# Turning x earlier, loading q's last blocks last, and two passes of the last w_out in a fused attention and MLP kernel

## The chip, the cores and the metric

The kernel runs on one core of a Trainium2 chip. The time is that of one execution on the device in microseconds (us); medians are over the runs of one comparison. Ratios are the mean time of one kernel's runs over that of the other kernel's runs of the same rounds, so not quite the ratio of the medians that I quote. The granted TensorE clock (the share of full speed that the chip allowed) is quoted where it bears on a reading.

## The reference, cut to what matters

```python
# attention, per batch of 8 and head of 8, S = 576, D = 64
r = np.maximum(x, 0.0);  phi = concat([r * cos, r * sin], axis=-1)     # for q and for k
kv  = einsum('bhsf,bhsd->bhfd', k_p, v);  z = sum(k_p, axis=2)
num = einsum('bhsf,bhfd->bhsd', q_p, kv); den = q_p . z + 1e-6
x   = (num / den) transposed to 4608 tokens x 512
# MLP
h = x @ w_in                       # 512 x 2048
g = h * (1 / (1 + exp(-beta * h)))
return g @ w_out                   # 2048 x 512
```

## The kernel before: the parts that matter

The MLP runs in 9 chunks of 512 tokens, each of 32 slots: in slots 0 to 15 a first product h (four matmuls of 512 columns, 0.86 us) and its Silu, in slots 16 to 31 four matmuls of the second product o. The attention of a later batch runs between the slots. Chunk 0 shares its time with batch 1, chunk 1 with batch 2. A batch has 9 blocks of 64 rows times 2 groups of four heads (pairs 0 and 1 in the code). For batch 1 the first seven blocks go through TensorE during chunk 0, and the last two (blocks 7 and 8) in chunk 1. VectorE scales v by cos and sin (`vb`), rectifies q and k, and divides num (`xs`, called x below). Every engine works through its own instructions in program order.

```python
# start, batch 0, pair 1 (cuts marked ...)
    kv_mm(0, 1, 6)
    kv_take((1,), 6, eng="act")
    x_mul(got, 0, 7)
    x_mul_act(got2, 7)
    warm_pe(1, bank=1)                       # filler product
    for n in range(7):
        num_mm(n, 1, 0, n)
    num_mm(7, 1, 6, 0)                       # writes banks 6 and 7
    ...                                      # w_in 0 cast by GpSimd, half of it by VectorE below
    x_turn_pe(0, 0, 8, 2, jps=(0,))
    got = x_rden(0, 0, 0, 7, (1,))
    x_mul(got, 0, 4)
    x_mul(got, 4, 7)
    x_mul(x_rden(6, 0, 7, 8, (1,)), 7, 8)    # reads banks 6 and 7
    warm_pe(3, bank=3)
    x_turn_pe(0, 0, 4, 4, ("act",), (1,))
    h_mm(0, 0, (0, 1))
    x_turn_pe(0, 4, 8, 5, ("act",), (1,))
    for jt in range(1, 4):
        h_mm(0, jt, (0, 1))                  # jt 2 and 3 write banks 6 and 7
...
# what runs between the slots of a chunk, batch b
        u = [
            (0, lambda: num_rest() if b == 2 else None),     # batch 1's blocks 7 and 8
            (0, lambda: (q_relu(b, 0), q_relu(b, 1), q_turn_dma(b), load_next())),
            (1, lambda: v_scale(b, 0)),
            (4, lambda: k_relu(b)),
            (6, lambda: v_scale(b, 1)),
            (7, lambda: q_tan(b, 0)),
            (8, lambda: q_tan(b, 1)),
            (12, lambda: (kv_mm(b, 0, 6), kv_mm(b, 1, 6), kv_take((0, 1), 6))),
        ]
```

## Time and profile before

| | before |
|---|---|
| median of the first 3 runs | 296.25 us (296.04 to 296.49) |
| span of the profiled execution | 294.3 us |
| TensorE / VectorE / ScalarE / GpSimd busy | 284.1 / 116.6 / 140.1 / 73.8 us |
| slot 4 of chunk 0 starts | 22.21 us |
| chunk 1's first product | 51.59 us |
| kv product of batch 2 starts / the h after it | 64.52 / 65.66 us |

TensorE is the bound: it has next to no idle time after 16 us. The rest is read by asking what TensorE waits for at a few places; the prediction shows those lines. One caution on this trace: some matmul records are missing from it, 28 of 3074 by the page's count of products and weight loads.

### The profile page before, as it was taken

The numbers are of one execution on the slowest core, as the hardware profiler recorded it, in microseconds if no ns is written. First come the engines' busy times: TensorE is split into PE (matmuls) and PEld (weight loads), VectorE is DVE, ScalarE is ACT, GpSimd is POOL, SyncE is SP. The second block draws the span as 40 slices with busy tenths as digits, with TensorE's granted clock in tenths as the row PEclk, the third lists the DMA queues.
The fourth block names the chain that finished last, engine by engine and source line by source line (L and its number), as shares of the span: only waits on it lengthen the run. The fifth ranks groups of instructions, "written<-read, shape, count | busy, mean of one in ns | idle before, by whom it ended". The sixth has DMA issues, their size and how long they took to land.

```text
span 294.3 us, 7183 instructions
## 1 busy us (share of the span) xinstructions
PE 284.1 (97%) x3046; PEld 143.2 (49%) x3074; DVE 116.6 (40%) x297; ACT 140.1 (48%) x223; POOL 73.8 (25%) x88
## 2 busy tenths in 40 slices
PE   8799999999999999999999999999999999999995
PEld 7454455455444544454444544554455444444444
DVE  5989968662920294009500860077005000000000
ACT  5768826572248214831384128511761177127611
POOL 1350003252382026402460156014701210000000
PEclk9999999999999999999999999999999999999999
DMA  7999999597898089925992599239201910131033
GB/s 258 373 391 381 389 390 391 192 286 275 159 280 348 2 110 222 374 86 111 210 392 79 102 226 379 82 63 181 64 2 33 159 37 0 38 71 36 0 73 72
DMA packets 50416, 53.82 MB, mean 183 GB/s; under 512 B 30912, under 2 KB 31312, under 8 KB 50384
## 3 DMA queue, kind: packets, MB, share of 16 engines
q1 hardware_dynamic: 47424, 45.88, 51.7%
q0 software_dynamic: 2688, 7.34, 10.1%
q8 instruction: 24, 0.39, 0.5%
q10 hardware_dynamic: 272, 0.14, 0.2%
q14 instruction: 8, 0.07, 0.1%
HBM read 36.71 MB, written 9.44 MB: 157 GB/s over the span
## 4 chain that ended last, share of the span: by engine, by line
PE 84%; DVE 5%; DMA 5%; ACT 2%; issue 2%
PE ps L366 38%; PE ps L391 37%; DMA w_stage<-in_moe_w_out_dram 5%; DVE win L108 4%; PE ps L281 4%; PE ps L260 3%; PE ps L406 1%; PE ps L415 1%; ACT vb L213 1%; DVE qs L218 1%; DVE xs L303 0%; ACT g_t L373 0%; ACT rk L188 0%; PE ps L424 0%; PE ps L230 0%
## 5 line engine op out<-in xcount | busy, mean ns | idle before, releaser
L366 PE MATMUL ps<-xt,win 128*128 128x512 bf16 x576 | 128.1, 379 | 0.7 <-ACT g_t L373 0.5
L391 PE MATMUL ps<-wout,g_t 128*128 128x512 bf16 x535 | 120.4, 379 | 2.5 <-issue 1.4
L373 ACT ACTIVATE g_t<-ps,beta 128x512 bf16<-128x512 f32 x144 | 98.5, 688 | 36.5 <-PE ps L366 36.5
L366 PEld LDWEIGHTS <-win 128*128 128x128 bf16 x576 | 55.3, 98 | 67.5 <-DVE win L108 1.4
L391 PEld LDWEIGHTS <-g_t 128*128 128x128 bf16 x560 | 54.0, 98 | 64.0 <-issue 0.5
L386 POOL DMA_DIRECT2D out_dram<-o_sb x56 | 36.5, 656 | 142.2 <-ACT o_sb L397 142.2
L397 ACT COPY o_sb<-ps 128x512 f32<-128x512 f32 x35 | 20.5, 587 | 98.2 <-PE ps L391 98.2
L218 POOL TENSOR_TENSOR qs<-qt,tanr 128x1152 bf16<-128x1152 bf16 x12 | 29.2, 2456 | 10.3 <-DVE vb L215 8.9
L272 DVE CAST kv<-ps 128x520 bf16<-128x520 f32 x6 | 4.2, 699 | 67.8 <-PE ps L260 67.8
L409 DVE COPY o_sb<-ps 128x256 f32<-128x256 f32 (+1 forms) x2 | 0.7, 358 | 62.6 <-PE ps L406 62.6
L303 DVE TENSOR_TENSOR xs<-ps,rden 128x768 bf16<-128x768 f32 (+5 forms) x26 | 23.1, 890 | 0.8
L292 DVE TENSOR_TENSOR den<-ps,eps 128x12 f32<-128x12 f32 (+4 forms) x26 | 4.2, 161 | 33.5 <-PE ps L281 33.5
L215 DVE TENSOR_SCALAR vb<-raw_v,cos 128x256 bf16<-128x256 f32 x63 | 17.1, 348 | 0.0
L215 DVE TENSOR_SCALAR vb<-raw_v,sin 128x256 bf16<-128x256 f32 x54 | 14.7, 350 | 0.0
L281 PEld LDWEIGHTS <-qt 64*64 64x64 bf16 x576 | 10.6, 106 | 5.0 <-issue 4.3
L281 PE MATMUL ps<-kv,qt 64*64 64x65 bf16 x576 | 11.8, 194 | 0.4 <-ACT kv L270 0.2
L190 DVE TENSOR_SCALAR qb<-raw_q 128x1152 bf16<-128x1152 f32 x16 | 11.4, 753 | 1.3 <-DMA raw_q<-in_q_dram 1.3
L108 DVE CAST win<-w_stage 64x512 bf16<-64x512 f32 (+1 forms) x28 | 11.6, 413 | 0.6
L281 PE MATMUL ps<-kv,qs 64*64 64x65 bf16 x576 | 11.6, 193 | 0.0
L260 PE MATMUL ps<-vb,rk 64*64 64x130 bf16 x576 | 10.0, 218 | 1.6 <-ACT rk L188 1.6
L260 PEld LDWEIGHTS <-rk 64*64 64x64 bf16 x576 | 8.5, 106 | 5.6 <-issue 3.0
L281 PEld LDWEIGHTS <-qs 64*64 64x64 bf16 x576 | 10.4, 105 | 0.0
(56 smaller groups left out, 99.3 us busy)
## 6 DMA issues: line engine op xcount, KB each, us to landing
raw_v<-in_v_dram SPq DMA_DIRECT2D x7, 1152.0 KB, 10.3
raw_k<-in_k_dram SPq DMA_DIRECT2D x7, 1152.0 KB, 12.7
raw_q<-in_q_dram SPq DMA_DIRECT2D x7, 1152.0 KB, 7.5
out_dram<-o_sb POOLq DMA_DIRECT2D x56, 128.0 KB, 4.0
w_stage<-in_moe_w_out_dram SPq DMA_DIRECT2D x4, 1024.0 KB, 9.1
w_stage<-in_moe_w_in_dram SPq DMA_DIRECT2D x3, 1024.0 KB, 13.0
out_dram<-o_sb SPq DMA_DIRECT2D x14, 128.0 KB, 2.3
raw_q<-in_q_dram SPq DMA_DIRECT2D x2, 576.0 KB, 4.4
```

Of the source, the lines that this page charges most:

```text
L108: nc.vector.tensor_copy(o, a)
L190: nc.vector.tensor_scalar(dst, src, scalar1=0.0, scalar2=None, op0=ALU.max)
L215: nc.vector.tensor_scalar(o, a, scalar1=t[:, n : n + 1], scalar2=None, op0=ALU.mult)
L218: eng.tensor_tensor(dst.rearrange("q n (g p) -> q n g p", g=2), src.rearrange("q n (g p) -> q n g p", g=2), tanr[:, n0:n1].unsqueeze(2).to ...
L260: nc.tensor.matmul(t[jj * HP : (jj + 1) * HP, g], lhsT=rk[hs, n, 2 * jp + jj, :], rhs=vb[hs, n, 2 * jp + jj].rearrange("q s e -> q (s e)") ...
L281: nc.tensor.matmul(ps[cols, bank + jj, slot * E : (slot + 1) * E], lhsT=(qt, qs)[cs][rows, jp, n, cols], rhs=kv[rows, g, jp, cs, :], start ...
L303: nc.vector.tensor_tensor(o.rearrange("q j n s d -> q j (n s) d"), nv[:, :, a:z, :, 0:D].rearrange("q j n s d -> q j (n s) d"), rden[:, :, ...
L366: nc.tensor.matmul(ps[:, h_bank(c, jt)], lhsT=win[jt // 4][:, mi, (jt % 4) * P : (jt % 4 + 1) * P], rhs=xt[:, :, jp, g * HP : (g + 1) * HP ...
L373: nc.scalar.activation(g_t, ps[:, h_bank(c, jt)], AF.Silu, scale=beta[:, jt : jt + 1])
L386: eng.dma_start(out=out_v[bb, n][:, m0:m1], in_=o_sb[hf * HP : (hf + 1) * HP, m0:m1])
L391: nc.tensor.matmul(o_ps, lhsT=gs[c, jt][:, tt * P : (tt + 1) * P], rhs=wout[jt // 4][:, jt % 4, :], start=(jt == 0), stop=(jt == JT - 1))
L397: nc.scalar.copy(o_sb, o_ps)
```

## The change

The intent is to shorten the start and the transition to chunk 1, where TensorE waits. It has three parts: the start (A), the late blocks of batch 1's q (B) and the last w_out in two passes (C).

```diff
 # A: the start
-    v_scale(0, 1, 0, 0, 6, eng="pool")          # and the rest of the 9 blocks on ScalarE
+    v_scale(0, 1, 0, 0, 8, eng="pool")
...
-    warm_pe(1, bank=1)
+    x_turn_pe(0, 0, 8, 4, jps=(0,))             # ahead of num of pair 1
     for n in range(7):
         num_mm(n, 1, 0, n)
...
-    for gj in GJ:
-        cast_win(0, gj, "pool", jps=slice(0, 1))
...
-    x_turn_pe(0, 0, 8, 2, jps=(0,))
+    for gj, eng in zip(GJ, ("pool", "pool", "dve", "pool")):
+        cast_win(0, gj, eng, jps=slice(0, 1))
+    for gj, eng in zip(GJ, ("dve", "pool", "pool", "pool")):
+        cast_win(0, gj, eng, jps=slice(1, 2))
...
-    warm_pe(3, bank=3)
+    warm_pe(2, bank=3)
+    h_mm(0, 0, (0, 1))
+    h_mm(0, 1, (0, 1))
     x_turn_pe(0, 0, 4, 4, ("act",), (1,))
-    h_mm(0, 0, (0, 1))
+    h_mm(0, 2, (0, 1))
+    h_mm(0, 3, (0, 1))
     x_turn_pe(0, 4, 8, 5, ("act",), (1,))
...
+            if slot == 0:
+                for jt in range(4):
+                    h_mm(0, jt, (2, 3), slice(0, 4))   # left column half of all four h first
+            h_mm(0, slot, (2, 3), slice(4, 8))
-            h_mm(0, slot, (2, 3))
             h_act(0, slot)
 # B: the late blocks of batch 1's q
-        load_raw(1, "q")
+        load_raw(1, "q", n1=7)
         load_w("out", 3)
+        load_raw(1, "q", n0=7)
...
+        d = 4 if b == 2 else 0                          # every batch: slots 0, 1, 4, 6, 7, 8 become d + 0, 1, 3, 5, 6, 7
+        if b == 2:
+            u = [(0, lambda: (q_relu(1, 0, n0=7), q_relu(1, 1, n0=7))), (2, q_rest), (4, num_rest)] + u
 # C: the last w_out in two passes, slots 28 to 31 of chunk 0
+            for tt in (2 * (slot % 2), 2 * (slot % 2) + 1):
+                o_mm(0, tt, range(12, 14) if slot < 30 else range(14, 16))
...
-                     [takes[0](*t) for t in turns], cast_wout(3, "addd"),
+                     [takes[0](*t) for t in turns], cast_wout(3, "adda"),    # ScalarE casts its last part too
```

For batch 2 part B moves the units some four slots later. For every later batch, where d is 0, it also moves the last four one slot earlier (k's rectification, the sin half of `vb` and the two tan products, slots 3, 5, 6 and 7 instead of 4, 6, 7 and 8).

More of the change, by code (lines that the diff above doesn't have):

```diff
@@ L73, in raw_tile, with load_raw @@
         return raws[name, b]
-    def load_raw(b, name, j0=0, j1=4):
-        js = slice(j0, j1)
+    def load_raw(b, name, j0=0, j1=4, n0=0, n1=NQ):
+        js, nd = slice(j0, j1), slice(n0 * D, n1 * D)
         src = {"q": q, "k": k, "v": v}[name][b]
         nc.sync.dma_start(
-            out=raw_tile(b, name)[:, js].rearrange("q j n d -> q j (n d)"),
-            in_=src.rearrange("(j g) (p n) d -> (g p) j (n d)", g=2, n=NQ)[:, js, :])
+            out=raw_tile(b, name)[:, js].rearrange("q j n d -> q j (n d)")[:, :, nd],
+            in_=src.rearrange("(j g) (p n) d -> (g p) j (n d)", g=2, n=NQ)[:, js, nd])
     win = [const.tile([P, MI, 512], BF16, name=f"win{i}") for i in range(4)]
@@ L190, in relu, with q_relu @@
             nc.vector.tensor_scalar(dst, src, scalar1=0.0, scalar2=None, op0=ALU.max)
-    def q_relu(b, jp, eng="dve"):
-        relu(qb[:, jp].rearrange("q n (j d) -> q j n d", j=2), raw_tile(b, "q")[:, 2 * jp : 2 * jp + 2], eng)
+    def q_relu(b, jp, eng="dve", n0=0, n1=NQ):
+        relu(qb[:, jp, n0:n1].rearrange("q n (j d) -> q j n d", j=2),
+             raw_tile(b, "q")[:, 2 * jp : 2 * jp + 2, n0:n1], eng)
     def k_relu(b, j0=0, j1=4, eng="dve", n0=0, n1=NQ):
@@ L220, in tan_mul, with q_turn_pe @@
             tanr[:, n0:n1].unsqueeze(2).to_broadcast([P, n1 - n0, 2, HP]), op=ALU.mult)
-    def q_turn_pe(b, jp, bank, hold=False):
-        parts = ((0, 0, 5), (1, 5, NQ))
+    def q_turn_pe(b, jp, bank, hold=False, parts=((0, 0, 5), (1, 5, NQ))):
         v2 = []
@@ L360, in h_bank, with h_mm @@
         return ((3, 2, 6, 7), (2, 3, 0, 1))[c][jt] if c < 2 and jt < 4 else HB[jt % 4]
-    def h_mm(c, jt, mis=range(4)):
+    def h_mm(c, jt, mis=range(4), blocks=slice(0, NB)):
         xt = xt_tile(c)
@@ L365, in h_mm @@
             jp, g = divmod(mi, 2)
-            nc.tensor.matmul(ps[:, h_bank(c, jt)],
+            nc.tensor.matmul(ps[:, h_bank(c, jt), blocks.start * 64 : blocks.stop * 64],
                              lhsT=win[jt // 4][:, mi, (jt % 4) * P : (jt % 4 + 1) * P],
-                             rhs=xt[:, :, jp, g * HP : (g + 1) * HP],
-                             start=(mi == 0), stop=(mi == MI - 1))
+                             rhs=xt[:, blocks, jp, g * HP : (g + 1) * HP],
+                             start=(mi == 0), stop=(mi == MI - 1 and blocks.stop == NB))
     def h_act(c, jt):
@@ L386, in store, with o_mm @@
             eng.dma_start(out=out_v[bb, n][:, m0:m1], in_=o_sb[hf * HP : (hf + 1) * HP, m0:m1])
-    def o_part(c, tt, part):
+    def o_mm(c, tt, jts):
         o_ps = ps[:, (2, 3, 0, 1)[tt] if c == 0 else 2 + tt % 2]
-        for jt in range(4 * part, 4 * part + 4):
+        for jt in jts:
             nc.tensor.matmul(o_ps, lhsT=gs[c, jt][:, tt * P : (tt + 1) * P],
@@ L393, in o_part @@
                              start=(jt == 0), stop=(jt == JT - 1))
-        if part < 3:
+        if jts[-1] < JT - 1:
             return
@@ L398, in o_part @@
         store(c, tt, o_sb)
+    def o_part(c, tt, part):
+        o_mm(c, tt, range(4 * part, 4 * part + 4))
     def o_last(c, tt):
@@ L442 @@
     take("dve", 1)
-    v_scale(0, 1, 0, 0, 6, eng="pool")
+    v_scale(0, 1, 0, 0, 8, eng="pool")
     take("act", 1)
-    v_scale(0, 1, 0, 6, NQ, eng="act")
+    v_scale(0, 1, 0, 8, NQ, eng="act")
     v_scale(0, 0, 0)
@@ L467 @@
     kv_mm(0, 1, 6)
+    x_mul_act(got2, 7)
     kv_take((1,), 6, eng="act")
     x_mul(got, 0, 7)
-    x_mul_act(got2, 7)
-    warm_pe(1, bank=1)
+    x_turn_pe(0, 0, 8, 4, jps=(0,))
     for n in range(7):
@@ L474 @@
     num_mm(7, 1, 6, 0)
-    for gj in GJ:
-        cast_win(0, gj, "pool", jps=slice(0, 1))
-    for gj in GJ:
-        cast_win(0, gj, "pool", 0, 256, slice(1, 2))
-    x_turn_pe(0, 0, 8, 2, jps=(0,))
+    for gj, eng in zip(GJ, ("pool", "pool", "dve", "pool")):
+        cast_win(0, gj, eng, jps=slice(0, 1))
+    for gj, eng in zip(GJ, ("dve", "pool", "pool", "pool")):
+        cast_win(0, gj, eng, jps=slice(1, 2))
     got = x_rden(0, 0, 0, 7, (1,))
@@ L483 @@
     x_mul(x_rden(6, 0, 7, 8, (1,)), 7, 8)
-    warm_pe(3, bank=3)
+    warm_pe(2, bank=3)
+    h_mm(0, 0, (0, 1))
+    h_mm(0, 1, (0, 1))
     x_turn_pe(0, 0, 4, 4, ("act",), (1,))
-    h_mm(0, 0, (0, 1))
+    h_mm(0, 2, (0, 1))
+    h_mm(0, 3, (0, 1))
     x_turn_pe(0, 4, 8, 5, ("act",), (1,))
-    for jt in range(1, 4):
-        h_mm(0, jt, (0, 1))
-    for gj in GJ:
-        cast_win(0, gj, "dve", 256, 512, slice(1, 2))
     def cast_halves(i):
@@ L516, in rest @@
         cast_wout(2)
-        q_relu(1, 0)
+        q_relu(1, 0, n1=7)
     def num_seven(jp, bank):
@@ L524 @@
     takes = []
+    SEVEN = ((0, 0, 4), (1, 4, 7))
     turns = (("act", 0), ("dve", 1), ("act", 1), ("dve", 0))
@@ L529 @@
         15: lambda: v_scale(1, 1, eng="act"),
-        22: lambda: (kv_mm(1, 0, 6), kv_mm(1, 1, 6), kv_take((0, 1), 6, "act"), q_relu(1, 1)),
-        25: lambda: takes.append(q_turn_pe(1, 0, 4, hold=True)),
-        26: lambda: (takes.append(q_turn_pe(1, 1, 6, hold=True)),
-                     [takes[0](*t) for t in turns], cast_wout(3, "addd"),
+        22: lambda: (kv_mm(1, 0, 6), kv_mm(1, 1, 6), kv_take((0, 1), 6, "act"), q_relu(1, 1, n1=7)),
+        25: lambda: takes.append(q_turn_pe(1, 0, 4, hold=True, parts=SEVEN)),
+        26: lambda: (takes.append(q_turn_pe(1, 1, 6, hold=True, parts=SEVEN)),
+                     [takes[0](*t) for t in turns], cast_wout(3, "adda"),
                      [takes[1](*t) for t in turns]),
@@ L540, with q_rest @@
     }
+    def q_rest():
+        for jp in range(2):
+            take = q_turn_pe(1, jp, (4, 7)[jp], hold=True, parts=((0, 7, NQ),))
+            take("act", 0)
+            take("dve", 0)
     def num_rest():
@@ L554, in load_next @@
                     load_raw(b + 1, name)
+        d = 4 if b == 2 else 0
         u = [
-            (0, lambda: num_rest() if b == 2 else None),
-            (0, lambda: (q_relu(b, 0), q_relu(b, 1), q_turn_dma(b), load_next())),
-            (1, lambda: v_scale(b, 0)),
-            (4, lambda: k_relu(b)),
-            (6, lambda: v_scale(b, 1)),
-            (7, lambda: q_tan(b, 0)),
-            (8, lambda: q_tan(b, 1)),
+            (d, lambda: (q_relu(b, 0), q_relu(b, 1), q_turn_dma(b), load_next())),
+            (d + 1, lambda: v_scale(b, 0)),
+            (d + 3, lambda: k_relu(b)),
+            (d + 5, lambda: v_scale(b, 1)),
+            (d + 6, lambda: q_tan(b, 0)),
+            (d + 7, lambda: q_tan(b, 1)),
             (12, lambda: (kv_mm(b, 0, 6), kv_mm(b, 1, 6), kv_take((0, 1), 6))),
         ]
+        if b == 2:
+            u = [(0, lambda: (q_relu(1, 0, n0=7), q_relu(1, 1, n0=7))), (2, q_rest), (4, num_rest)] + u
         u.append((18, lambda: (num_all(0, 4), num_all(1, 6), num_all(2, 0))))
@@ L576 @@
             h_group(0, slot)
-        else:
-            o_part(0, slot % 4, (slot - 16) // 4)
+        elif slot < 28:
+            o_part(0, slot % 4, (slot - 16) // 4)
+        else:
+            for tt in (2 * (slot % 2), 2 * (slot % 2) + 1):
+                o_mm(0, tt, range(12, 14) if slot < 30 else range(14, 16))
         if slot == 24:
```

## The prediction

> **What bounds the kernel now.** I read the page first, for which engine fills the span.
>
> ```profile
> span 294.3 us, 7183 instructions
> PE 284.1 (97%) x3046; PEld 143.2 (49%) x3074; DVE 116.6 (40%) x297; ACT 140.1 (48%) x223; POOL 73.8 (25%) x88
> L366 PE MATMUL ps<-xt,win 128*128 128x512 bf16 x576 | 128.1, 379 | 0.7 <-ACT g_t L373 0.5
> L391 PE MATMUL ps<-wout,g_t 128*128 128x512 bf16 x535 | 120.4, 379 | 2.5 <-issue 1.4
> ```
>
> TensorE (PE) is busy 97% of the span, nearly all in the two large products. The change adds no such product and removes none. The chain of waits shows 64 first products in one piece of 13.81 us, 216 ns each. So the change can only win at places where PE stands still, and must lose where it makes PE stand still. All of PE's idle time is 294.3 - 284.1 = 10.2 us, most of it before 16 us; a gain of 2% (5.9 us) is out of reach.
>
> Next I read the chain of waits in order of time, around the first batch change, 44 to 66 us. Columns: start, duration, what.
>
> ```profile
> 31.44 13.76 DMA w_stage<-in_moe_w_out_dram
> ...
> 45.22 0.73 ACT wout L115
> ...
> 45.99 1.02 PE ps L391 x4
> ...
> 50.62 0.92 ACT xt L345
> ...
> 51.59 1.02 PE ps L366 x4
> ...
> 55.27 1.27 ACT g_t L373 x2
> ...
> 56.59 7.93 PE ps L366 x36
> 64.52 1.15 PE ps L260 x72
> ```
>
> PE waits shortly three times: for the last w_out quarter (landed 45.20, cast by ScalarE 45.22 to 45.94, used 45.99), for the turned x of batch 1 (51.59), and for a PSUM bank that a Silu still reads (56.59). The list of waits gives 0.22, 0.23 and 0.49 us: together 0.94 us. The last line is the kv product of batch 2, in PE's order after slot 12 of chunk 1.
>
> Third, busy time by stretch, for the DMA. Columns: stretch, its length, busy time of five engines, clock, DMA share, GB/s.
>
> ```profile
> 30.00:35.00 5.00, 4.95 (x24) 2.16 (x24) 4.91 (x14) 4.20 (x9) 0.00 (x0) 1.00 1.04 392
> 40.00:45.00 5.00, 4.84 (x60) 2.90 (x51) 3.26 (x6) 1.87 (x3) 0.00 (x0) 1.00 1.05 388
> ```
>
> From 5 to 50 us the DMA engines are full at 360 to 400 GB/s: the 45.20 landing is a matter of bytes queued ahead, not of when the load is issued.
>
> Fourth, VectorE's timeline from batch 1's last blocks to batch 2's kv product.
>
> ```profile
> 54.80 0.17 DVE L292 TENSOR_TENSOR den<-ps,eps 128x8 f32<-128x8 f32 x1 [1.14 <-PE ps L281]
> 55.24 0.69 DVE L303 TENSOR_TENSOR xs<-ps,rden 128x512 bf16<-128x512 f32 x1
> 55.85 1.42 DVE L190 TENSOR_SCALAR qb<-raw_q 128x1152 bf16<-128x1152 f32 x2
> 57.18 2.45 DVE L215 TENSOR_SCALAR vb<-raw_v,cos 128x256 bf16<-128x256 f32 x9
> 59.55 1.35 DVE L190 TENSOR_SCALAR rk<-raw_k 128x2304 bf16<-128x2304 f32 x1
> 60.81 2.45 DVE L215 TENSOR_SCALAR vb<-raw_v,sin 128x256 bf16<-128x256 f32 x9
> 65.71 0.70 DVE L272 CAST kv<-ps 128x520 bf16<-128x520 f32 x1 [2.45 <-PE ps L260]
> ```
>
> VectorE waits for the num product of batch 1's last two blocks (PE 54.24 to 54.63), then prepares batch 2 without a pause until 63.26. PE takes that at 64.45, so the slack is only 1.19 us.
>
> **What the Trainium skill says.** "TensorE: Matmul & The Clock Gate", section "Wait — 56ns, not 53.3ns?": back-to-back matmuls of 512 columns start 215.7 ns apart when warm. The trace agrees (216 ns). The same page, "HAM oscillation — how this bites in real kernels", warns of idle gaps above about 3.4 us; the trace has none and I expect none, so I add no clock loss. "PSUM — Partial Sum Buffer", "PSUM bank collisions raise a hardware error", says to guard PSUM by bank and that even two reads collide. The trace agrees: ScalarE's copy of qt waits for VectorE's qs from the same bank (four times, 1.7 us in all). "DMA: Bandwidth & Descriptors", "Specifications", gives about 358 GB/s of HBM per core; the trace moves up to 400, so I use the trace.
>
> **The change, part by part.**
>
> *Start (16 to 22 us).* The eight turns of pair 0 go ahead of num 1, where one filler of 0.39 us stood. They wait for VectorE's x (14.35 + 1.08 = 15.43) and take some 0.45 us, so num 1 starts at about 15.95 instead of 15.65, 0.3 us later; VectorE's chain to x of block 7, which ended at 18.59, ends at about 18.9. It has 0.93 us idle before that chain, enough for the two casts it now takes (64x512, 0.42 each). PE gains four real products in the filler's place, but product 2 writes bank 6, which x of block 7 still reads: PE stands until about 18.95. Then come 4 products (0.86), 4 turns (0.25), and two passes of eight half-width products (0.86 each): end at about 21.8, against 21.9 before. So on PE this is worth 0.1 us. On VectorE four casts of w_in 0 vanish (18.59 to 20.06): the later casts run some 1.1 us earlier, and PE's four waits for them, which cost about 0.05 us of a product each pair of slots, go: 0.3 us more. PE comes to slot 28 about 0.4 us earlier, and 0.2 us more because 14 blocks are turned instead of 18 (55 ns each): 45.77 becomes about 45.1.
>
> *Loading order.* Two ninths of batch 1's q go behind the last w_out: 1.18 MB x 2/9 = 0.26 MB, at 390 GB/s 0.67 us. It lands at about 44.55; with the same 0.72 us cast PE starts slot 28 at about 45.33 (45.99 before), a gain of 0.66 us. This wait, not the start, is the limit there, so the start's gain is not added.
>
> *w_out in two passes.* Slots 28 to 31 have the same 16 products, the last casts needed later. But two output copies now stand just ahead of the xt copy on ScalarE: ready about 49.25, 0.5 each, then 0.91, so PE starts chunk 1 at about 51.15 instead of 51.59. The gain falls to about 0.4 to 0.5 us.
>
> *Late blocks.* Their turn moves to after slot 2, num to after slot 4, and batch 2's work on VectorE stands behind them in program order. New timeline: slot 0 done at about 53.7 (54.24 before); slots 1 to 3 are 1.3 us and the four turns 0.2, so 55.25; slot 4 waits for its bank to about 55.85 and ends at 56.7; num waits for VectorE's half of the turned q until about 56.75. Before it began at 54.24: VectorE's chain starts 2.5 us later. From num's start to the end of the last vb takes 63.26 - 54.24 = 9.0 us, so kv of batch 2 can start at about 65.8. PE, with num (0.4) and eight slots (6.9) after 56.75, is there at 64.1. It stands still for 1.7 us. kv starts at 65.8 instead of 64.45: **1.35 us lost**, with the earlier gains already counted in. After that every step has slack: the tan products on GpSimd ended at 67.85 for a num at 70.88, both move by like amounts, and chunks 2 to 8 are unchanged.
>
> Sum: 296.25 + 1.35 = 297.6. I set **297.4 us**, since the loading part may win a little more than I count.
>
> **Rivals.** (1) *VectorE has more room than I think, and kv does not wait.* Then the earlier 0.5 us survives with the 0.49 us bank wait: about 295.3. For it: somebody placed the units at slots 4 to 11 on purpose. Against: 9.0 us of VectorE work does not fit in eight slots of 0.863 us plus 0.4. (2) *The gain is larger, the start paying in full*: if w_out landed early enough, slot 28 would start near 45.1 and kv would still wait for VectorE: 297.2. (3) *Splitting q costs bandwidth*: rows fall from 2304 to 1792 and 512 bytes; if the loads slow, w_out lands as late as before and the total is 298.2. Nothing in this trace separates these row sizes. (4) *The start gets slower*: casts block num's chain if the second half of w_in 0 lands after 16.2 us (an estimate: 0.52 MB after 14.85 us). Cast slack and the w_out wait hide this unless it is over 0.7 us.
>
> **Range and chances.** The kv wait is arithmetic on measured durations; its error is mostly the gain before it, from nothing to about 1.2 us: 296.1 to 298.5. Both verdicts beyond 2% need nearly 6 us, several times any term: 1% faster, 2% slower.
>
> **What would show it.** In the changed trace: w_out landing about 44.5; slot 28 near 45.3; chunk 1 near 51.15; VectorE unbroken from num's end to a last vb near 65.8; PE idle about 1.7 us before kv of batch 2, put down to VectorE's vb; chunk 2 about 1.3 us later than before, and the same distance to the end. I am wrong if kv starts below 64.4, if PE has no such wait, or if it grows past 3 us and the clock falls.

## The result, and the profile after

The changed kernel took 298.39 us (298.00 to 299.60, 6 runs), the kernel before 296.14 us (295.67 to 296.78, 6 runs) in the same rounds. The ratio is 1.0079, with a 95% interval of 1.0057 to 1.0101: slower by a little under 1%.

The page of the changed kernel, the same two lines as before:

```profile
span 296.2 us, 7226 instructions
PE 287.3 (97%) x3080; PEld 144.5 (49%) x3080; DVE 116.5 (39%) x298; ACT 139.9 (47%) x224; POOL 73.6 (25%) x86
```

The busy totals say nearly nothing: the same work, and TensorE still at 97%. (Its busy time rises by 3.2 us mainly because this trace lacks no product.) The chain of waits at the transition says more (start, duration, what):

```profile
51.52 1.02 PE ps L366 x4
...
57.19 0.48 PE ps L281 x32
57.67 7.01 PE ps L366 x32
64.68 0.54 PE ps L260 x16
...
66.28 0.76 PE ps L260 x40
67.04 2.70 PE ps L366 x12
```

Chunk 1 starts at 51.52, 0.07 us earlier than before. The kv product of batch 2 (L260) starts at 64.68, about as before, but its 72 matmuls take until 67.04 instead of 65.66. In the second cut stand four pieces of 0.25 us with four matmuls each. VectorE's timeline shows what paces them (start, duration, instruction, in brackets idle time before it and its cause):

```profile
56.41 0.76 DVE L219 TENSOR_TENSOR qs<-ps,tanr 128x256 bf16<-128x256 bf16 x2 [2.34 <-ACT qt L235]
57.76 0.17 DVE L292 TENSOR_TENSOR den<-ps,eps 128x8 f32<-128x8 f32 x1 [0.59 <-PE ps L281]
...
63.77 2.46 DVE L216 TENSOR_SCALAR vb<-raw_v,sin 128x256 bf16<-128x256 f32 x9
```

The nine scaled blocks of v come from 63.77 to 66.23, and the kv product follows them block by block. This is a wait that hardly looks like one: TensorE's records there are "busy", and the list of waits gives only 0.4 us (its weight load, for vb). The change in duration, 1.15 to 2.36 us, is the sign. VectorE idled 2.34 and 0.59 us just before, behind the late blocks of batch 1.

That is 1.38 us. The profiled executions differ by 2.01 us at their last copies (290.84 and 292.85), so something comes later. (The medians differ by 2.25; the profiled run, 298.00 us, is the quickest of its six.) The start of the kv product of each further batch, from the chains of waits, shows where:

| kernel | batch 3 | batch 4 | batch 5 | batch 6 | batch 7 | steps between them |
|---|---|---|---|---|---|---|
| before | 94.97 | 125.32 | 155.66 | 186.00 | 216.35 | 30.35, 30.34, 30.34, 30.35 |
| changed | 96.24 | 126.88 | 157.22 | 187.57 | 218.36 | **30.64**, 30.34, 30.35, **30.79** |

Chunks 2 and 5 are longer by 0.30 and 0.44 us. The change touches them only by the one slot by which part B moves VectorE's and GpSimd's units, and that is not the cause: start_only and before_plus12 below have the old slots and both pauses, late_only has the new slots and no pause in chunk 2. The chain of the changed kernel has a pause in each, "for issue", that is, for nothing that the trace shows:

```profile
104.03 1.83 PE ps L391 x8
105.86 0.12 issue
105.99 9.67 PE ps L391 x44
...
194.00 1.33 PE ps L281 x134
195.32 0.26 issue
195.58 0.23 PE ps L281 x4
```

Both stand at the num product (L281) or two groups of products behind it.

At the start TensorE's own list of waits has two new entries (sum, times, longest):

```profile
PE ps L281 <- ACT g_t L373: 0.7, 1, 0.7
PE ps L366 <- DVE xs L303: 0.6, 1, 0.6
```

Slot 4 of chunk 0 starts at 22.99 instead of 22.21.

### The profile page after: what moved, and what is told of

Read it like the earlier page. It is cut to its first block, busy times and chain, and to the rows that moved or that the text cites. A ratio compares the mean times of both kernels' runs of the same rounds, so it can differ in the third digit from the quotient of the medians. Undisturbed runs are those within 1.5% of the kernel's fastest.

```text
span 296.2 us, 7226 instructions
## 1 busy us (share of the span) xinstructions
PE 287.3 (97%) x3080; PEld 144.5 (49%) x3080; DVE 116.5 (39%) x298; ACT 139.9 (47%) x224; POOL 73.6 (25%) x86
## 3 DMA queue, kind: packets, MB, share of 16 engines
q0 software_dynamic: 2688, 7.34, 10.2%
## 4 chain that ended last, share of the span: by engine, by line
PE 91%; DMA 3%; DVE 2%; ACT 2%; issue 1%; SPq 1%
PE ps L366 41%; PE ps L391 41%; PE ps L281 4%; PE ps L260 3%; DMA raw_v<-in_v_dram 3%; PE ps L409 1%; ACT g_t L373 1%; SPq L78 1%; DVE xs L303 1%; PE ps L340 0%; ACT o_sb L397 0%; DVE rden L296 0%; ACT xt L345 0%; DVE vb L206 0%; PE ps L230 0%
## 5 line engine op out<-in xcount | busy, mean ns | idle before, releaser
L366 PE MATMUL ps<-xt,win 128*128 128x512 bf16 (+1 forms) x584 | 128.1, 376 | 1.3 <-DVE xs L303 0.6
L391 PE MATMUL ps<-wout,g_t 128*128 128x512 bf16 x560 | 124.6, 379 | 0.1
L366 PEld LDWEIGHTS <-win 128*128 128x128 bf16 x584 | 56.4, 98 | 66.8 <-issue 2.0
L281 PEld LDWEIGHTS <-qt 64*64 64x64 bf16 x576 | 10.6, 106 | 5.2 <-issue 4.3
L260 PE MATMUL ps<-vb,rk 64*64 64x130 bf16 x576 | 11.3, 219 | 1.6 <-ACT rk L188 1.4
L281 PE MATMUL ps<-kv,qt 64*64 64x65 bf16 x576 | 11.8, 194 | 0.9 <-ACT g_t L373 0.7
L260 PEld LDWEIGHTS <-rk 64*64 64x64 bf16 x576 | 8.9, 106 | 6.5 <-ACT rk L188 2.4
L190 DVE TENSOR_SCALAR qb<-raw_q 128x1152 bf16<-128x1152 f32 (+2 forms) x18 | 11.8, 690 | 0.7 <-DMA raw_q<-in_q_dram 0.7
L281 PE MATMUL ps<-kv,qs 64*64 64x65 bf16 x576 | 11.7, 193 | 0.3 <-issue 0.3
L108 DVE CAST win<-w_stage 64x512 bf16<-64x512 f32 x26 | 11.0, 423 | 1.0 <-DMA w_stage<-in_moe_w_in_dram 0.4
L281 PEld LDWEIGHTS <-qs 64*64 64x64 bf16 x576 | 10.5, 105 | 0.4 <-issue 0.4
## 6 DMA issues: line engine op xcount, KB each, us to landing
raw_v<-in_v_dram SPq DMA_DIRECT2D x7, 1152.0 KB, 10.2
```

The costliest lines, as they stand in the source:

```text
L108: nc.vector.tensor_copy(o, a)
L190: nc.vector.tensor_scalar(dst, src, scalar1=0.0, scalar2=None, op0=ALU.max)
L260: nc.tensor.matmul(t[jj * HP : (jj + 1) * HP, g], lhsT=rk[hs, n, 2 * jp + jj, :], rhs=vb[hs, n, 2 * jp + jj].rearrange("q s e -> q (s e)") ...
L281: nc.tensor.matmul(ps[cols, bank + jj, slot * E : (slot + 1) * E], lhsT=(qt, qs)[cs][rows, jp, n, cols], rhs=kv[rows, g, jp, cs, :], start ...
L366: nc.tensor.matmul(ps[:, h_bank(c, jt), blocks.start * 64 : blocks.stop * 64], lhsT=win[jt // 4][:, mi, (jt % 4) * P : (jt % 4 + 1) * P], ...
L391: nc.tensor.matmul(o_ps, lhsT=gs[c, jt][:, tt * P : (tt + 1) * P], rhs=wout[jt // 4][:, jt % 4, :], start=(jt == 0), stop=(jt == JT - 1))
```

## The experiments

Theory V says that the loss is VectorE's chain: batch 2's preparation now stands behind the late blocks. Rival S says that it comes from the start, and rival P that it comes from ScalarE's two output copies in part C. The two late pauses raised a further question, taken up in the second set (theory F and rival G).

### First set: each part alone, and the wait taken away

**late_only**: the kernel before with part B alone (the other hunks undone).

> Kernel before plus only the late blocks of batch 1's q (load split, their turn after slot 2, their num after slot 4, batch 2's preparation on VectorE four slots later). Theory V (VectorE is late for batch 2's kv): a wait of 1.3 to 1.8 us at kv of batch 2, total 1.0 to 1.4 us above before, about 297.3. Rival S (the loss comes from the start, where ScalarE holds num 8 back by 0.7 us): this kernel is at before or up to 0.5 us below, 295.7 to 296.2, without a wait at kv.

Measured: 296.96 us (5 runs) against 296.16 (11 runs, shared by this set), ratio 1.0029 (1.0017 to 1.0041). Chunk 1 starts at 51.15, 0.44 us earlier than in before. The h after kv of batch 2 starts at 66.67, 1.01 us later than in before. So B alone gains nearly half a microsecond early and loses 1.45 us by the end of kv. One small step of 0.19 us stands in chunk 5. Theory V holds; rival S does not explain this kernel.

**start_only**: the kernel before with part A alone.

> Kernel before plus only the new start (x of pair 0 ahead of num 1, casts on two engines, h by column halves, one scaled v more on GpSimd). Theory V: TensorE comes to slot 4 some 0.5 to 0.8 us later than in before, of which the wait for the last w_out hides 0.2, so 0.2 to 0.5 us above before, about 296.5. Rival S: 1.4 us or more above before.

Measured: 297.42 us (6 runs), ratio 1.0045 (1.0030 to 1.0061). This is more than theory V expected. It is less than rival S asked for, but the interval (0.9 to 1.8 us) reaches that; the trace separates the two. At the h after kv it is only 0.15 us behind before (65.81 against 65.66). The rest comes in chunks 2 and 5, whose steps are 30.83 and 31.01 us. The new start costs 0.15 us by the waits that one can name, and about 1.15 us by pauses 80 and 170 us later.

**two_pass_only**: the kernel before with part C alone.

> Kernel before plus only the last w_out in two passes. Theory V: within 0.2 us of before, 296.0 to 296.4; chunk 1 starts within 0.2 us of 51.6. Rival P (the two output copies ahead of the x copy on ScalarE cost the time): 0.7 us or more above before.

Measured: 296.27 us (5 runs), ratio 0.9999 (0.9986 to 1.0012). Chunk 1 started at 52.00, 0.4 us later than expected, but in this execution q of batch 1 landed late: TensorE waited 0.63 us for it at 43.58. The time is level, so C costs nothing measurable and rival P falls. Alone, the three parts lose 0.80, 1.26 and 0.11 us by the medians, together 2.17 of the 2.25 us of the whole.

**vcos_first**: the changed kernel with one edit. VectorE idles after slot 0 of chunk 1, so the cos half of batch 2's `vb` can go there, ahead of the late blocks.

```diff
-            (d + 1, lambda: v_scale(b, 0)),
+            (1, lambda: v_scale(b, 0)),
```

> The changed kernel with one edit: the cos half of batch 2's scaled v goes to VectorE after slot 1, ahead of batch 1's late blocks, where VectorE idles 2.3 us. Theory V: the wait at kv of batch 2 (2.4 us of trickling product instead of 1.15) goes, total 1.1 to 1.4 us below the changed kernel, about 297.1. If the loss has another cause: no change, 298.4.

Measured: 297.05 us (5 runs), ratio 1.0034 to before (1.0022 to 1.0047), so 1.3 us below the changed kernel's 298.39. VectorE's timeline:

```profile
54.05 2.49 DVE L216 TENSOR_SCALAR vb<-raw_v,cos 128x256 bf16<-128x256 f32 x9
56.47 0.76 DVE L219 TENSOR_TENSOR qs<-ps,tanr 128x256 bf16<-128x256 bf16 x2
...
61.47 2.45 DVE L216 TENSOR_SCALAR vb<-raw_v,sin 128x256 bf16<-128x256 f32 x9
65.94 0.70 DVE L272 CAST kv<-ps 128x520 bf16<-128x520 f32 x1 [2.01 <-PE ps L260]
```

The cos half fills the idle time without moving what follows it (56.47 against 56.41), the sin half is ready at 63.92, and kv runs from 64.74 in 1.15 us. The wait is gone and the time falls by what it cost. The two steps in chunks 2 and 5 stay (30.59 and 30.80).

### Second set: the pauses in chunks 2 and 5

In the first set both pauses appear in the three kernels that have part A (changed, start_only, vcos_first), after num products that do not depend on it. Part A changes one thing for the whole rest of TensorE's stream: its length. The half-width passes add 8 products and 8 weight loads, and two fillers with their loads are dropped: 12 instructions more. The pages agree, with 3080 weight loads, one for each product, instead of 3074: 6160 instructions instead of 6148.

The Trainium skill has a place on this: "Runtime: NRT & Kernel Launch", section "Instruction fetch mechanics". An engine's instructions are refilled in blocks of 16 KiB, 256 instructions, by the sequencer's own DMA queue, and the cost of crossing a block boundary is "mostly hidden". The page of the kernel before agrees on the size:

```profile
q8 instruction: 24, 0.39, 0.5%
```

That is 24 packets in 0.39 MB, 16 KB each; 24 blocks of 256 are 6144 instructions, about TensorE's stream. The trace of the changed kernel bears out that this is TensorE's queue: from the start of its first packet to that of its last, TensorE has 5827 records, 253 for each packet, and no other engine has more than 411 in all. One num product of a batch has 288 small instructions in 1.36 us, more than a block. Theory F: a pause occurs where the next block is asked for too shortly ahead of such a burst, and twelve instructions move these places. Rival G: the pauses come from data or DMA that the new start shifted. A cheap way to move the stream is the 58 small filler products at the very beginning.

```diff
-    warm_pe(58, 48)
+    warm_pe(64, 48)      # before_plus12;  52 in start_minus12 and after_minus12
```

**before_plus12**: the kernel before with six fillers more, nothing else.

> The kernel before with 64 instead of 58 of those fillers: 12 more TensorE instructions, nothing else. Theory F: pauses of 0.3 to 0.7 us appear in chunks 2 and 5 and the total rises by 0.5 to 1.2 us, to about 297.1. Rival G: 296.2, no pause.

Measured: 297.49 us (6 runs) against 295.96 (11 runs), ratio 1.0049 (1.0035 to 1.0062), with all runs between 297.07 and 297.75. The chain has both pauses, at the places where the changed kernel has its own:

```profile
103.00 1.83 PE ps L391 x8
104.84 0.40 issue
105.24 4.91 PE ps L391 x22
...
193.24 1.33 PE ps L281 x133
194.57 0.71 issue
195.28 0.22 PE ps L281 x3
```

The steps of chunks 2 and 5 are 30.91 and 31.25 us, together 1.46 us over before, nearly the whole loss of this kernel (1.53 by the medians); at the kv of batch 2 it is only 0.18 us behind. No load, no operand and no order of anything else was changed. The fillers do shift the rest in time by some tenths, but late_only shifts these chunks by 0.9 us with no pause in chunk 2 and 0.19 us in chunk 5. Rival G falls: the start is the old one here. What is shown is that twelve more instructions make these pauses; that TensorE waits there for an instruction block is a reading.

**start_minus12**: start_only with six fillers fewer.

> The kernel with the new start alone (297.42 us), with six of the 58 small filler products at the very beginning taken out: 12 TensorE instructions fewer, so that the rest of its stream has the same place in the 256-instruction blocks as in before. Theory F (the two pauses of 0.49 and 0.67 us in chunks 2 and 5 are waits for an instruction block, whose place moved by 12): both pauses go, about 1.1 us less, 296.3. Rival G (the pauses come from data, semaphores or DMA that the new start shifted): no change, 297.4.

Measured: 299.59 us (5 runs), ratio 1.0119: a miss, in the other direction. The two old pauses do shrink to one of 0.32 us in chunk 5, but a much larger one appears at 14.6 us, inside the kv product of batch 0. TensorE's timeline:

```profile
13.96 0.64 PE L260 MATMUL ps<-vb,rk 64*64 64x130 bf16 x20 [0.51 <-ACT rk L188]
17.02 0.65 PE L260 MATMUL ps<-vb,rk 64*64 64x130 bf16 x16 [2.42 <-issue]
```

TensorE stops after 20 of 36 matmuls for 2.42 us, for nothing that the trace shows. An instruction packet starts at 14.75 in this execution; in the kernels without this pause the corresponding one starts at 9.6 to 10.4. After the pause the granted clock was 0.50 from 16 to 20 us, and the mean clock of these runs is 0.989 to 0.994, which adds to the loss.

**after_minus12**: the changed kernel with six fillers fewer.

> The changed kernel with 52 instead of 58 fillers. Theory F: its pauses of 0.30 and 0.45 us go, 0.5 to 0.8 us less than the changed kernel, about 297.7, with the wait at kv of batch 2 (2.4 us of trickling product) left as it was. Rival G: 298.4.

Measured: 300.65 us (297.32 to 301.26, 6 runs), ratio 1.0142: a miss for the same reason. The pause at 14.6 us is 2.71 us here. One of the six runs, at a clock of 0.999, took 297.32 us, near the 297.7 that theory F expected; the other five, at 0.989 to 0.994, took over 300.5. That run was not profiled, so whether it lacked the early pause is not known. But the question that it was made for is answered by its trace: kv of batches 3 to 7 starts at 99.51, 129.85, 160.20, 190.54 and 220.89, in steps of 30.34 or 30.35 us. The pauses of chunks 2 and 5 are gone, while the trickling kv of batch 2 is as in the changed kernel.

One more regularity ties the pauses to the instruction packets. Every gap of TensorE that stands for issue alone in the traces after 14 us, from 0.12 to 2.71 us (the 0.16 us of missing records aside), ends 2.3 to 2.7 us after a packet of the instruction queue started, for example 103.61 and 105.98 in the changed kernel, 102.53 and 105.24 in before_plus12, 14.75 and 17.02 in start_minus12. When TensorE asks for a block, I can't see in a trace, and most of the 24 packets are followed by no pause, so I can't say ahead of a run where one will fall.

**best**: the changed kernel with cos v first, a different order at the start, the second half of the first h in full width, and 60 fillers.

```diff
-    h_mm(0, 2, (0, 1))
-    h_mm(0, 3, (0, 1))
     x_turn_pe(0, 4, 8, 5, ("act",), (1,))
+    h_mm(0, 2, (0, 1))
+    h_mm(0, 3, (0, 1))
...
-            if slot == 0:
-                for jt in range(4):
-                    h_mm(0, jt, (2, 3), slice(0, 4))
-            h_mm(0, slot, (2, 3), slice(4, 8))
+            h_mm(0, slot, (2, 3))
```

> The changed kernel with cos v of batch 2 first, x of blocks 4 to 7 turned ahead of the products that wait for the same x, the second half of the first h in full width again, and 60 fillers (the same number of TensorE instructions as before). Theory: the Silus begin 0.6 us earlier than in the changed kernel, num 8's wait of 0.7 us for ScalarE goes, slot 4 starts near 22.3 instead of 22.99; kv of batch 2 does not wait; no pauses: about 296.0, so 2.4 us below the changed kernel. If the half-width passes were not what held the Silus back: slot 4 stays at 23.0 and the total near 296.4.

Measured: 295.75 us (295.30 to 297.80, 6 runs) against 295.96, ratio 1.0002 (0.9978 to 1.0026). The profiled execution is the slow one of the six (clock 0.994): TensorE stood 1.55 us for ScalarE's k at 14.85 and ran at a granted clock of 0.62 from 16 to 20 us. It says nothing on slot 4. A pause of 0.57 us stands in chunk 5, although this kernel has as many instructions as before: the count alone does not decide where pauses fall.

### Third set: a larger dose, and two repaired versions

**late_six**: late_only with the late blocks two slots later.

```diff
-        d = 4 if b == 2 else 0
+        d = 6 if b == 2 else 0
-            u = [..., (2, q_rest), (4, num_rest)] + u
+            u = [..., (4, q_rest), (6, num_rest)] + u
```

> The kernel with the late blocks alone (296.96 us), with their turn after slot 4 instead of 2, their num after slot 6 instead of 4, and batch 2's VectorE work behind it. Theory V (kv of batch 2 starts 9.0 us after that num, whatever TensorE does): two slots are 1.73 us, the wait at kv grows by as much, so some 298.6. Rival (the cost of the late blocks is their two small bank waits and extra turns, not VectorE's chain): 297.0.

Measured: 300.23 us (6 runs), in two groups. Three runs at full clock took 299.13 to 299.54, 2.2 us above late_only, where theory V expected 1.7; 0.3 us of the difference is there before chunk 1 in the profiled execution (the kv product of batch 1 at 39.70 against 39.36). Three runs at a clock of 0.994 took 300.93 to 301.44. In the profiled one, of the second group, kv waits and then follows VectorE block by block, and after it TensorE runs at half rate for a while:

```profile
66.64 3.28 PE L260 MATMUL ps<-vb,rk 64*64 64x130 bf16 x72 [1.24 <-DVE vb L216]
69.86 3.32 PE L366 MATMUL ps<-xt,win 128*128 128x512 bf16 x9
```

Nine products in 3.3 us are far from 0.216 us each; six of them in a row start 0.40 to 0.43 us apart. So the wait grows with the number of slots, as V says, and in this execution it cost the clock as well: it was 0.67 from 69 to 74 us.

**late_two_vcos**: parts B and C with cos v first, and the old start.

> The changed kernel with the old start and with cos v of batch 2 first. TensorE has as many instructions as in before. Theory V and F: no wait at kv of batch 2, chunk 1 starts near 51.15, kv ends near 65.4 against 65.66 in before, no pauses or only one of 0.2 us: 295.8 to 296.2, level with before. If the old start was not the other part of the loss: above 296.8.

Measured: 295.95 us (5 runs) against 296.00 (11 runs), ratio 0.9990 (0.9969 to 1.0011). kv of batch 2 runs from 64.22 in 1.15 us, 0.3 us earlier than in before, and a pause of 0.39 us in the step after it gives that back (kv of batch 3 at 94.95 against 94.97). Without part A and without the wait at kv, nothing of the loss is left.

**turn_full**: the kernel best with 58 fillers.

> The kernel called best with 58 fillers instead of 60: four TensorE instructions fewer than before, the early part of the stream as in the changed kernel. Theory F: the pauses of the changed kernel after num of chunks 2 and 5 are changed or gone, since 16 instructions less stand ahead of them. Slot 4 near 22.4 instead of 22.99, since the Silus start earlier; no wait at kv. With no pause 295.3; with one of 0.6 us 295.9.

Measured: 295.77 us (295.66 to 297.10, 6 runs; one of them at a clock of 0.994) against 296.00, ratio 0.9999 (0.9975 to 1.0023). The start, in TensorE's timelines; first the changed kernel:

```profile
20.12 1.91 PE L366 MATMUL ps<-xt,win 128*128 128x256 bf16 x16
22.99 3.63 PE L366 MATMUL ps<-xt,win 128*128 128x512 bf16 x16
```

and then turn_full:

```profile
19.52 2.75 PE L366 MATMUL ps<-xt,win 128*128 128x512 bf16 x12
22.59 3.63 PE L366 MATMUL ps<-xt,win 128*128 128x512 bf16 x16
```

Slot 4 starts at 22.59, although everything before it was 0.4 us later in this execution (the kv product of pair 1 at 14.91 against 14.50): from there to slot 4 it takes 7.68 us instead of 8.49. The first Silu comes 0.8 us earlier relative to that kv product (21.02 against 21.42), and num 8's wait of 0.7 us for its Silu is gone; the wait for x ahead of the products is 0.25 us instead of 0.57. So the order at the start held the Silus back. This run changes two things there, the full width and the earlier turns of blocks 4 to 7, and no run separates them. There is no pause in chunks 2 and 5 (steps of 30.34 and 30.35), and no wait at kv. The profiled execution is 0.4 us shorter than that of before, 293.9 us against 294.3; the timed rounds don't separate the two kernels. It is 2.6 us faster than the changed kernel by the medians, and level with the one before. No version here is shown to beat the kernel before.

## Why the prediction was right or wrong

*What bounds the kernel.* Right. TensorE stays at 97%, and each part can be followed by where TensorE stands. The 10.2 us of idle time were too many, since the records missing from that trace count as idle: the second product shows 120.4 us there and 124.6 us in the changed kernel, for the same work. Some 6 us remain, an estimate from these numbers, so a gain of 2% was out of reach all the more.

*The late blocks.* Right in mechanism, and in size partly by luck. The prediction gave 1.35 us at kv of batch 2; the trace shows 1.38 at its end, vcos_first took 1.3 us away with one moved line, and late_six made it grow. VectorE's chain from num to the last vb took 9.04 us, as predicted (9.0). Two details differ. The num of the late blocks started at 57.19 instead of 56.75, and the last vb ended at 66.23 instead of 65.8. And TensorE does not stand still for 1.7 us in front of kv: it starts at 64.68 and trickles, so that kv ends 0.81 us after the last vb instead of its own 1.15. The chain's 0.43 us of lateness and these 0.34 us nearly cancel; late_only, without the late start, ends kv only 1.01 us behind before. The expected sign, an idle TensorE with VectorE named as the releaser, was therefore hardly there.

*The start.* Wrong in sign, though small. "So on PE this is worth 0.1 us" and "PE comes to slot 28 about 0.4 us earlier" became 0.78 us later at slot 4 (22.99 against 22.21) and 0.47 us later at kv of batch 1 (39.60 against 39.13). The stand before product 2 was there: it lasted 0.57 us and ended at 19.04, where I had 18.95. What I left out is on ScalarE. With half-width passes over all four h, no h is complete before the second pass; the first Silu began at 21.42 instead of 20.64, and num 8, which needs the bank of the second h, waited 0.7 us for its Silu. turn_full shows that this is a matter of the order of products and turns: it takes 0.8 us less over that stretch.

*The loading order.* That the wait for w_out goes was right, and in late_only, without the new start, chunk 1 begins 0.44 us earlier, as predicted for the whole change (0.4 to 0.5). The agreement is partly luck: late_only has no part C, whose copies were to reduce 0.66 to that number. Its gain is what the wait (0.22 us) and four turns less ahead of slot 28 (about 0.22) are worth. In the changed kernel the late start ate it: TensorE came to slot 28 at about 46.0, as in before, so a w_out that had landed by 44.98 had nothing to give. Chunk 1 began at 51.52 instead of the predicted 51.15. Here was also rival 4 to be seen: VectorE's second cast waited 0.42 us for the second half of w_in 0 and began at 16.31, as estimated at 16.2, and moved num's chain by no more than 0.1 us.

*"Chunks 2 to 8 are unchanged."* This step failed, and with it "The change adds no such product": the work is the same, but eight products are split in two, and the prediction had no term for a longer stream. The two pauses add 0.30 and 0.44 us, that is 0.74 of the 0.99 us between the predicted 297.4 and the measured 298.39. Another 0.2 us are what the prediction took off its sum of 297.6 for a gain by the loading, which did not come. The sum in the profile is 1.38 at kv, less 0.11 us that before itself lost between there and kv of batch 3 (65.66 to 94.97, against 67.04 to 96.24), plus 0.74: 2.01, as seen at the end.

*Range and chances.* The range held, at its upper end, and for a reason not in it: the width was meant for the gain ahead of kv, and was used up by pauses that no term stood for.

What stays open: whether TensorE does wait for an instruction block in these pauses, and if so, which place in the stream makes it ask too late. Moving the stream by 12 instructions made pauses (before_plus12) and removed them (after_minus12), but kernels of the same length differ (best has one of 0.57 us, after_minus12 none).

## What to carry to other kernels

When work moves later on the bound engine, follow what stands behind it in program order on the helper engines, and count that chain against the slots left: a gain of half a microsecond was bought with a VectorE chain that came 1.4 us too late, and one line moved into VectorE's idle time repaired it. Look for waits in durations too, since a product that follows its operand block by block shows as busy. And when a change of a few instructions moves the time of stages it does not touch, add a dozen idle instructions to the kernel before: here that alone cost 1.5 us, so an edit should be judged by the stage that it touches before its total is believed.

## What the Trainium skill lacked or had wrong

- "Runtime: NRT & Kernel Launch", "Instruction fetch mechanics", calls the cost of crossing a 16 KiB boundary mostly hidden. If the pauses here are such boundaries, as their timing suggests, the cost is exposed in several variants of this unrolled kernel: 0.2 to 0.9 us in the steps of later chunks, and 2.42 and 2.71 us at 14.6 us in start_minus12 and after_minus12. Each ended 2.3 to 2.7 us after an instruction packet started. No page says how to tell from a trace at which instruction the next block is asked for.
- "TensorE: Matmul & The Clock Gate", "HAM oscillation — how this bites in real kernels", asks for no idle gaps above about 3.4 us. Here shorter gaps among the small products of batch 0 were followed by a lower granted clock from 16 to 20 us: 2.42 us by 0.50 (start_minus12), 2.71 us by 0.63 (after_minus12) and 1.55 us by 0.62 (best); 0.92 us at the same place was not (turn_full, 1.00). In late_six, a 1.24 us gap and a thinly fed kv product of 3.3 us were followed by 0.67 from 69 to 74 us; three of its six runs had a mean clock of 0.994.
